# A normalised-attention and two-layer kernel on one core: the SBUF pools put in another order and padded by 832 bytes, so that most large tiles start at a multiple of 2,048 bytes

## The chip, the cores and the metric

The kernel runs on one core of a Trainium2 chip. The metric is the device time of one execution in microseconds (us). TensorE is called PE here, its loading of the stationary operand PEld, VectorE DVE, ScalarE ACT, GpSimd POOL, and SyncE, which issues the transfers, SP. SBUF is the core's working memory: 128 partitions, and a tile has the same byte address in each of them. The addresses of this document are bytes within a partition.

## The reference, cut to what matters

```python
# q, k, v: (4, 6080, 256) float32; w_in (256, 2048), w_out (2048, 256) float64
qn = q / (norm(q, axis=1) + 1e-06)
kn = k / (norm(k, axis=1) + 1e-06)
a = softmax(kn.transpose(0, 2, 1) @ qn / tau)     # 256 x 256 for each of 4 batches
x = (v @ a).reshape(24320, 256)
h = x @ w_in
out = (h - tanh(h)) @ w_out                       # 24320 x 256
```

## The kernel before, in words

**Arithmetic.** The 256 x 256 matrix `a` of a batch is multiplied into `w_in` ("fold", `ps_w`, 12 matmuls for each of 8 column blocks), so that only `v @ (a @ w_in)` is left. Every operand is kept as two float32r parts, a high one and the rest (`vh` and `vl` of v, `gh` and `gl` of h - tanh(h), `f[:, 0]` and `f[:, 1]` of the folded weights, `wo_h` and `wo_l` of `w_out`), and every product is three matmuls: high by rest, high by high, rest by high (`products`, line 267; the six calls of line 868 are two such products). The first two batches' scores `ps_s` are plain float32 matmuls of 256 columns, which the profile lists as two records each; those of batches 2 and 3 are float32r.

**Tiling.** A "quad" is two slices of 512 columns of v (480 in a batch's last pair) by 256 columns of the folded weights. There are 4 batches x 6 pairs x 8 blocks = 192 quads. One quad is a Strassen-like scheme of 7 products, 21 matmuls in which an `f` slice of 128 columns is the stationary operand and a `vh` or `vl` tile moves, and 4 results that each go through tanh, a subtraction and the split into `gh` and `gl`, and then through 6 matmuls with slices of `wo_h` and `wo_l` (24 in all): 45 matmuls. All 192 quads make 8,640, the folds 384, the float32r scores 576: 9,600 float32r matmuls of the 10,034 records on PE.

**Order.** A planner (`Plan.order`) fixes the order of the instructions on every engine from its own cost figures before anything is emitted; it knows rings of buffers (`Ring`), no addresses. `manual_schedule` emits that order. PE takes its matmuls in the written order (`ORDER`, `LAG`), and the other engines work ahead of it within the rings: 3 buffers for `f`, 8 for `vh` and `vl`, 5 for `gh` and `gl`, 3 for `u`, 4 for `c` and `t`, 2 for `ob`, `qh`, `ql` and `nt`, 3 for `raw` and `wi`. All transfers are issued by SP.

**Where tiles lie.** SBUF is handed out in the order in which pools are opened, and in a pool in the order in which tags are first used; each tile is rounded up to 32 bytes. In the program as built, `ident`, the first tile, is at byte 16,512. With tile sizes from the code, everything else follows:

| tiles (bytes each) | PE's use | before: bytes past a multiple of 2,048 | after |
|---|---|---|---|
| `wo_h`, `wo_l` (16,384) | stationary, slices of 512 bytes | 1,216 | 0 |
| `wi` x3 (4,096) | moving, 1,024 bytes | 1,216 | 0 |
| `f` x3 (7,168) | stationary, slices of 512 bytes | 1,216 / 192 / 1,216 | 0 / 1,024 / 0 |
| `raw` x3 (4,096) | first scores | 192 | 0 |
| `nt` x2 (3,040) | none | 192 / 1,184 | 1,024 / 2,016 |
| `qh`, `ql` x2 each (4,096) | both operands of the scores | 128 | 0 |
| `vh`, `vl` x8 each (2,048), `vraw`, `vt` (8,192) | `vh`, `vl` moving, 2,048 bytes | 128 | 0 |
| `eh`, `el` (2,048, in `sm_p`) | stationary in the folds | 352 | 1,184 |
| `u`, `gh`, `gl`, `ob`, `c`, `t` (2,048) | `gh`, `gl` moving, 2,048 bytes | 480 | 0 |

The first matmuls of the program also use `vh`, `vl`, `gh`, `gl`, `qh` and `ql` buffers as landing places for q and k, since these buffers are still empty.

Of the kernel before, what the change touches and what calls it, by code (L numbers as in the profile page):

```python
# [10 lines left out]
F32 = mybir.dt.float32  # L11
F32R = mybir.dt.float32r
I32 = mybir.dt.int32
# [5 lines left out]
P = 128  # L19
GJ = 2  # L20
NMAX = 512
NSQ = 760
# [12 lines left out]
ORDER = [  # L35
    ("p6", []), ("p2", [4, "c"]), ("p5", [2]), ("p7", [3, "a", 6]), ("p4", ["d"]), ("p1", [1]), ("p3", [4, "b", 4]),
]
LAG = 30


# [169 lines left out]
def attn_moe(ctx: ExitStack, tc: tile.TileContext, q, k, vT, qkT, tau, w_in, w_out, outT):  # L210
# [21 lines left out]
    SLOTS = NP * NS2  # L232
    TOTAL = B * SLOTS

    const = ctx.enter_context(tc.tile_pool(name="const", bufs=1))
    w_p = ctx.enter_context(tc.tile_pool(name="w_p", bufs=2))
    f_p = ctx.enter_context(tc.tile_pool(name="f_p", bufs=1))
    qk_p = ctx.enter_context(tc.tile_pool(name="qk_p", bufs=2))
    v_p = ctx.enter_context(tc.tile_pool(name="v_p", bufs=1))
    sm_p = ctx.enter_context(tc.tile_pool(name="sm_p", bufs=1))  # L240
    g_p = ctx.enter_context(tc.tile_pool(name="g_p", bufs=4))
    ps_p = ctx.enter_context(tc.tile_pool(name="ps_p", bufs=1, space=bass.MemoryType.PSUM))
    ring = {
        "wi": Ring(3), "f": Ring(3), "fx": Ring(1), "raw": Ring(3), "qh": Ring(2), "ql": Ring(2), "nt": Ring(2),
# [4 lines left out]
    def sb(pool, tag, shape, dtype, name):  # L249
        return pool.tile(list(shape), dtype, tag=tag, name=name, bufs=ring[tag].bufs)  # L250
# [23 lines left out]

    tau_sb = const.tile([1, 1], F32, name="tau_sb")
    itau = const.tile([P, 1], F32, name="itau")

    ps_tau = []

# [10 lines left out]
    WN = 512  # L290

    class Convert:
# [10 lines left out]
        def magnitude(self):  # L303
            words = self.raw.rearrange("p a (n w) -> p (a n) w", w=2)
            self.low, self.high = words[:, :, 0], words[:, :, 1]
            self.a = sb(qk_p, "nt", [P, NSQ], I32, f"a_{self.name}")[:, 0:WN]
            self.af = self.a.bitcast(F32)

            nc.scalar.activation(self.af, self.high.bitcast(F32), AF.Abs)
# [63 lines left out]
    class Attn:  # L373
# [107 lines left out]
        def load_channels(self, i):  # L481

            row, part = divmod(i, N // NSQ)
            self.channels[i] = sb(qk_p, "nt", [P, NSQ], F32, f"nt_{self.b}_{i}")
            nc.sync.dma_start(
                self.channels[i],
                qkT[row // KC, self.b, row % KC * P:(row % KC + 1) * P, part * NSQ:(part + 1) * NSQ],
            )
# [599 lines left out]
    current = None  # L1088
    lag = LAG

# [70 lines left out]
```

## Time and profile before

| | |
|---|---|
| median of 3 runs | 2247.32 us (2245.41 to 2250.69) |
| the profiled execution's own time | 2247.82 us |
| its span, first to last instruction | 2246.0 us |
| mean granted PE clock | 0.995 |
| PE, PEld, DVE, ACT, POOL busy | 98%, 81%, 78%, 68%, 4% |
| DMA engines busy with the kernel's own queue | 42.9% |

The profile comes from one execution. A group is all instructions of one line, engine, operation and shape, named by its tiles (result first). Matmuls overlap each other in the pipeline, so the length of one (394 ns) is not what it costs: that is the pitch, the time from one matmul's start to the next one's. The chain of waits follows the work that ended last back to the start.

### The profile page before, as it was taken

The page shows a single profiled execution, that of the slowest core. Times are in us where ns is not written, and L with a number is a line of the kernel's source. Part 1 is how long each engine was busy: PE and PEld are TensorE (multiplying, and loading weights), DVE is VectorE, ACT ScalarE, POOL GpSimd, SP SyncE. Part 2 cuts the span into 40 slices and gives each one's busy share as a digit, 9 for nine tenths or more (in the row PEclk, how much of TensorE's full clock was granted, in tenths as well). Part 3 has the DMA queues.
Part 4 walks back from the last instruction along what each step waited for, and adds up shares of the span by engine and source line. Part 5 has one row for each costly group of instructions (what it writes and reads, how often), then busy time and mean ns, then how long its engine had stood idle before and what let it go on. Part 6 is the DMA issues. An engine that isn't in the chain of part 4 may idle for free.

```text
span 2246.0 us, 28772 instructions
## 1 busy us (share of the span) xinstructions
PE 2209.2 (98%) x10034; PEld 1819.5 (81%) x10034; DVE 1750.7 (78%) x2813; ACT 1534.2 (68%) x2770; POOL 79.3 (4%) x62
## 2 busy tenths in 40 slices
PE   8899999999999999999999999999999999999999
PEld 6677778778888888888888888888888888888887
DVE  7688877778788777787788877777778877777775
ACT  6356777776677776776667767777667666666665
POOL 7222000000000000000000000000000000000000
PEclk9899999999999999999999999999999999999999
DMA  9763443443445444444335444444333333332331
GB/s 358 249 217 134 160 161 143 162 149 109 153 163 180 176 150 173 153 161 165 112 138 190 150 175 164 164 176 154 135 122 122 137 129 106 120 117 102 118 118 51
DMA packets 107379, 343.32 MB, mean 153 GB/s; under 512 B 11746, under 2 KB 17378, under 8 KB 107234
## 3 DMA queue, kind: packets, MB, share of 16 engines
q1 hardware_dynamic: 107234, 341.49, 42.9%
q8 instruction: 79, 1.29, 0.2%
q14 instruction: 66, 0.54, 0.1%
HBM read 282.98 MB, written 58.46 MB: 152 GB/s over the span
## 4 chain that ended last, share of the span: by engine, by line
PE 92%; DMA 4%; DVE 2%; issue 1%; ACT 1%; POOL 0%; SPq 0%; DVEq 0%; ACTq 0%; POOLq 0%
PE ps_o L868 46%; PE x L267 23%; PE y L267 11%; PE z L267 6%; PE ps_s L267 4%; PE ps_w L267 2%; DMA outT_dram<-ob 2%; DMA wi<-wi_d 1%; DMA vl<-k_dram 1%; DMA vh<-q_dram 0%; DVE ob L883 0%; DMA gh<-q_dram 0%; DMA vraw<-vT_dram 0%; DMA raw<-q_dram 0%; DMA raw_wi<-w_in_dram 0%
## 5 line engine op out<-in xcount | busy, mean ns | idle before, releaser
L868 PE MATMUL ps_o<-gh,wo_l 128*128 128x512 f32 (+1 forms) x1536 | 604.8, 394 | 4.4 <-DVE ob L883 4.3
L868 PE MATMUL ps_o<-gh,wo_h 128*128 128x512 f32 (+1 forms) x1536 | 605.3, 394 | 0.0
L812 DVE TENSOR_TENSOR gl<-t,gh 128x512 fp32r<-128x512 f32 (+1 forms) x768 | 513.2, 681 | 64.4 <-ACT gh L808 62.0
L808 ACT CAST gh<-t 128x512 fp32r<-128x512 f32 (+1 forms) x768 | 463.0, 618 | 85.1 <-DVE t L804 83.5
L267 PE MATMUL x<-vh,f 128*128 128x512 f32 (+1 forms) x1536 | 478.2, 392 | 1.2 <-DVE f L616 1.2
L868 PE MATMUL ps_o<-gl,wo_h 128*128 128x512 f32 (+1 forms) x1536 | 478.1, 392 | 0.0
L800 ACT ACTIVATE t<-c 128x512 f32<-128x512 f32 (+1 forms) x576 | 361.9, 629 | 166.5 <-DVE c L788 160.8
L804 DVE TENSOR_TENSOR t<-c,t 128x512 f32<-128x512 f32 (+1 forms) x576 | 397.0, 692 | 83.1 <-ACT t L800 73.9
L779 ACT COPY u<-x 128x512 f32<-128x512 f32 (+1 forms) x384 | 223.5, 582 | 235.8 <-PE x L267 235.3
L868 PEld LDWEIGHTS ps_o<-gh,wo_l 128*128 128x128 f32 x1536 | 288.3, 188 | 71.0 <-DVE ob L883 8.0
L267 PEld LDWEIGHTS x<-vh,f 128*128 128x128 f32 x1536 | 288.4, 188 | 66.4 <-DVE f L616 1.7
L868 PEld LDWEIGHTS ps_o<-gl,wo_h 128*128 128x128 f32 x1536 | 288.3, 188 | 61.8
L868 PEld LDWEIGHTS ps_o<-gh,wo_h 128*128 128x128 f32 x1536 | 288.6, 188 | 60.1
L788 DVE TENSOR_TENSOR c<-u,y 128x512 f32<-128x512 f32 (+1 forms) x384 | 260.4, 678 | 86.5 <-ACT u L779 47.4
L267 PE MATMUL x<-vl,f 128*128 128x512 f32 (+1 forms) x768 | 301.7, 393 | 2.1 <-ACT gh L808 1.2
L267 PE MATMUL y<-vh,f 128*128 128x512 f32 (+1 forms) x768 | 238.4, 391 | 0.0
L788 DVE TENSOR_TENSOR c<-p,z 128x512 f32<-128x512 f32 (+1 forms) x192 | 130.8, 681 | 98.9 <-PE z L267 96.9
L804 DVE TENSOR_TENSOR t<-x,t 128x512 f32<-128x512 f32 (+1 forms) x192 | 131.4, 684 | 74.0 <-ACT t L800 72.4
L800 ACT ACTIVATE t<-x 128x512 f32<-128x512 f32 (+1 forms) x192 | 114.0, 594 | 100.9 <-PE x L267 99.4
L267 PEld LDWEIGHTS x<-vl,f 128*128 128x128 f32 x768 | 144.1, 188 | 35.9 <-ACT gh L808 1.6
L267 PEld LDWEIGHTS y<-vh,f 128*128 128x128 f32 x768 | 144.0, 188 | 32.0
L267 PE MATMUL y<-vl,f 128*128 128x512 f32 (+1 forms) x384 | 150.9, 393 | 0.0
(119 smaller groups left out, 2021.8 us busy)
## 6 DMA issues: line engine op xcount, KB each, us to landing
f<-f_d SPq DMA_DIRECT2D x160, 896.0 KB, 4.6
nt<-qkT_dram SPq DMA_DIRECT2D x96, 380.0 KB, 5.6
f_d<-f SPq DMA_DIRECT2D x32, 896.0 KB, 4.5
vraw<-vT_dram SPq DMA_DIRECT2D x80, 256.0 KB, 5.8
outT_dram<-ob SPq DMA_DIRECT2D x80, 256.0 KB, 2.7
raw<-q_dram SPq DMA_DIRECT2D x73, 256.0 KB, 4.9
raw<-k_dram SPq DMA_DIRECT2D x73, 256.0 KB, 5.2
wi<-wi_d SPq DMA_DIRECT2D x30, 512.0 KB, 5.4
```

Source lines behind the costliest of these rows:

```text
L267: ins = nc.tensor.matmul(out, w, x, start=first and i == 0, stop=last and i == len(seq) - 1, skip_group_check=True,)
L779: nc.scalar.copy(self.tiles[to], self.tiles["X"][:, 0:self.n])
L788: nc.vector.tensor_add(self.tiles[i], self.tiles[u], self.tiles[ps][:, 0:self.n])
L800: nc.scalar.activation(self.tiles["t", i], self.tiles[c][:, 0:n], AF.Tanh)
L804: nc.vector.tensor_sub(x, self.tiles[c][:, 0:n], x)
L808: nc.scalar.copy(self.g[i][0], self.tiles["t", i])
L812: nc.vector.tensor_sub(self.g[i][1], self.tiles["t", i], self.g[i][0].bitcast(F32))
L868: nc.tensor.matmul(outs[key + (m,)][:, 0:n], (wo_l if part else wo_h)[:, f, m * P:(m + 1) * P], quad.g[i][x], start=first and j == 0, stop ...
```

## The change: the pools and their order

Three things are done. A tile of 208 float32 (832 bytes) that nothing uses is put behind `itau` in the first pool. The pools are opened in the order `const`, `w_p`, `v_p`, `g_p`, `qk_p`, `f_p`, `nt_p`, `sm_p`. And the tag `nt`, whose 3,040 bytes are no multiple of 2,048, moves out of `qk_p` into a pool of its own. 17,600 + 832 = 18,432 = 9 x 2,048 is then the address of `wo_h`, and the sizes of `w_p` to `fx` are all multiples of 2,048. The middle `f` buffer starts 1,024 bytes past one, because an `f` tile has 3.5 x 2,048 bytes. No instruction is added, removed or moved; no size or number of buffers changes. The last tile ends at byte 228,640 where it ended at 227,808.

```diff
+PAD = 208
...
     const = ctx.enter_context(tc.tile_pool(name="const", bufs=1))
     w_p = ctx.enter_context(tc.tile_pool(name="w_p", bufs=2))
+    v_p = ctx.enter_context(tc.tile_pool(name="v_p", bufs=1))
+    g_p = ctx.enter_context(tc.tile_pool(name="g_p", bufs=4))
+    qk_p = ctx.enter_context(tc.tile_pool(name="qk_p", bufs=2))
     f_p = ctx.enter_context(tc.tile_pool(name="f_p", bufs=1))
-    qk_p = ctx.enter_context(tc.tile_pool(name="qk_p", bufs=2))
-    v_p = ctx.enter_context(tc.tile_pool(name="v_p", bufs=1))
+    nt_p = ctx.enter_context(tc.tile_pool(name="nt_p", bufs=2))
     sm_p = ctx.enter_context(tc.tile_pool(name="sm_p", bufs=1))
-    g_p = ctx.enter_context(tc.tile_pool(name="g_p", bufs=4))
...
     itau = const.tile([P, 1], F32, name="itau")
+    const.tile([P, PAD], F32, name="pad")
...
-            self.a = sb(qk_p, "nt", [P, NSQ], I32, f"a_{self.name}")[:, 0:WN]
+            self.a = sb(nt_p, "nt", [P, NSQ], I32, f"a_{self.name}")[:, 0:WN]
...
-            self.channels[i] = sb(qk_p, "nt", [P, NSQ], F32, f"nt_{self.b}_{i}")
+            self.channels[i] = sb(nt_p, "nt", [P, NSQ], F32, f"nt_{self.b}_{i}")
```

## The prediction, made before the change was run

> **What bounds the kernel now.** I read the page's busy times first, then PE's waits, then the chain of waits, then stretches of the timeline of PE for the pitch, and last the groups and the transfers.
>
> ```profile
> span 2246.0 us, 28772 instructions
> PE 2209.2 (98%) x10034; PEld 1819.5 (81%) x10034; DVE 1750.7 (78%) x2813; ACT 1534.2 (68%) x2770; POOL 79.3 (4%) x62
> ```
>
> PE is idle for 2246.0 - 2209.2 = 36.8 us of the span, and every other engine has slack. What PE waits for (line, releaser, us in total, times, longest):
>
> ```profile
> PE ps_w L267 <- DMA wi<-wi_d: 11.0, 3, 5.0
> PE ps_s L267 <- DMA vl<-k_dram: 6.5, 5, 3.4
> PE ps_o L868 <- DVE ob L883: 4.3, 7, 1.0
> ```
>
> These are the three longest waits, 21.8 us together; the first two lie in the first 180 us. So time can come from PE's pitch, of which there are 9,600 of one kind, or from the start. The chain of waits (start, length, what) gives the pitch of a whole quad. One run of nine `ps_o` matmuls stands in each quad at the same place:
>
> ```profile
> 1803.52 2.10 PE ps_o L868 x9
> 1814.00 2.10 PE ps_o L868 x9
> 1824.49 2.10 PE ps_o L868 x9
> 1834.97 2.10 PE ps_o L868 x9
> ...
> 1950.33 2.10 PE ps_o L868 x9
> ```
>
> The first and the last are 14 quads apart: 146.81 / 14 = 10.486 us a quad, and 10.486 / 45 = 0.2330 us a matmul. So the 160 quads of 512 columns alone are 1,678 us, and a change of 1 ns in the pitch of the 9,600 float32r matmuls is 9.6 us, 0.43% of the span. That is the lever, and all that the change can pull on it is addresses.
>
> **The change part by part.** No instruction, transfer, wait or buffer is added or taken away: the planner knows no addresses, so the order on each engine stays, and the unused tile of 832 bytes issues nothing. The tag `nt` keeps its two buffers, so what waits for a free one stays too. These edits cost 0. What is left is whether an access is dearer or cheaper for the byte at which it starts. Before, nothing large starts at a multiple of 2,048 or even of 256, so the trace can't show the new case itself; but it has five comparisons between different starts.
>
> *First, the start of PE's stationary slices.* The three `f` buffers start 1,216, 192 and 1,216 bytes past a multiple of 2,048, and a quad takes the next one. Slices of 512 bytes that cross a 2,048-byte border in one buffer don't in the next. The four spacings above whose rows are shown are 10.48, 10.49 and 10.48 us, and the 14 of them average 10.486: at most 0.01 us a quad, 0.2 ns a matmul, hangs on the buffer. The rings of five for `gh` and `gl` and of eight for `vh` and `vl` turn as well. For `wo_h` and `wo_l` I take the end, where only `ps_o` is left (start, length, engine, line):
>
> ```profile
> 2233.76 0.38 PE L868 MATMUL ps_o<-gh,wo_l 128*128 128x480 f32 x1
> ...
> 2235.06 0.38 PE L868 MATMUL ps_o<-gh,wo_l 128*128 128x480 f32 x1
> ...
> 2236.37 0.38 PE L868 MATMUL ps_o<-gh,wo_l 128*128 128x480 f32 x1
> ...
> 2237.68 0.38 PE L868 MATMUL ps_o<-gh,wo_l 128*128 128x480 f32 x1
> ...
> 2238.98 0.38 PE L868 MATMUL ps_o<-gh,wo_l 128*128 128x480 f32 x1
> ```
>
> Each row opens a result's six matmuls. The results come in the order 12, 11, 22, 21, 12 here; those of row 1 read slices at 1,216 and 1,728 past a multiple (the second crosses the border), those of row 2 at 192 and 704 (neither does). The spacings are 1.30, 1.31, 1.31 and 1.30 us, with no step between the two kinds. Stationary slices: 0, bounds +-0.01 / 6 us, 1.7 ns, by the rounding of these rows, and +-0.2 ns by the quads.
>
> *Second, the start of PE's moving tiles, in plain float32.* In the first 45 us the scores come out of buffers of three kinds, warm and one after the other:
>
> ```profile
> 21.12 8.80 PE L267 MATMUL ps_s<-gh,gl 128*128 128x256 f32 x40
> 29.76 7.07 PE L267 MATMUL ps_s<-raw 128*128 128x256 f32 x32
> 36.66 5.34 PE L267 MATMUL ps_s<-vh,vl 128*128 128x256 f32 x24
> ```
>
> From start to start: (29.76 - 21.12) / 40 = 0.2160 us at 480 past, (36.66 - 29.76) / 32 = 0.2156 us at 128 past (these `raw` tiles lie in `qh` and `ql`). 352 bytes more or less: 0.4 ns or less.
>
> *Third, the same for float32r.* `vh` and `vl` move from 128 past, `gh` and `gl` from 480 past:
>
> ```profile
> 242.50 2.10 PE ps_o L868 x9
> 244.61 1.40 PE x L267 x6
> ```
>
> 2.10 / 9 and 1.40 / 6 are both 0.2333 us. The rounding of the rows leaves 0.6 + 0.8 = 1.4 ns between them. So a moving tile's start is worth 0, bounds +-1.4 ns on 9,600 matmuls, +-13.4 us. I take 0, because the two starts differ as much from each other as either does from the new one.
>
> *Fourth, both reads at the same place.* After the change stationary and moving operands mostly start at the same byte of a 512-byte stretch; before, they are 64 (`f`, `vh`) and 224 bytes apart (`wo_h`, `gh`). The scores of batches 2 and 3 have had equal starts all along (`qh` against `qh`, or `ql`, 0 apart), and the folds (`wi` at 1,216, `eh` at 352) have 160:
>
> ```profile
> 1007.02 0.28 PE L267 MATMUL ps_s<-ql,qh 128*128 128x256 f32 x1
> ...
> 1007.73 0.39 PE L868 MATMUL ps_o<-gh,wo_l 128*128 128x512 f32 x1
> ```
>
> ```profile
> 1165.02 0.40 PE L267 MATMUL ps_w<-wi,eh 128*128 128x256 f32 x2
> ...
> 1166.45 0.38 PE L868 MATMUL ps_o<-gh,wo_h 128*128 128x480 f32 x1
> ```
>
> 0.71 / 6 = 0.1183 us with equal starts, 1.43 / 12 = 0.1192 us with 160 between: 0.9 ns, and the rounding of the first alone is 1.7 ns. I take 0, bounds +-1.7 ns for 256 columns, so 3.4 ns for 512.
>
> [...]
>
> *Fifth, the other engines and the transfers.* Groups of DVE at three starts (line, tiles, shape, count, busy, mean ns):
>
> ```profile
> L812 DVE TENSOR_TENSOR gl<-t,gh 128x512 fp32r<-128x512 f32 x640 | 431.4, 687 | 53.5 <-ACT gh L808 51.3
> L674 DVE TENSOR_TENSOR vl<-vraw,vh 128x512 fp32r<-128x512 f32 x60 | 41.0, 684 | 0.0
> L463 DVE TENSOR_TENSOR ql<-raw,qh 128x1024 fp32r<-128x1024 f32 x46 | 56.2, 1222 | 6.7 <-ACT qh L456 6.6
> ```
>
> 687 ns with all three tiles at 480, 684 ns with all at 128. 512 columns more cost 535 to 538 ns at mixed starts (192 and 128). Bounds +-3 ns of 687. PE's work covers it: DVE idles 22% of the span; without that cover, 3 ns on 2,813 instructions would be 8 us. For transfers, the issues (tiles, queue, count, KB, median us to landing) and two stretches of the start (busy times of PE, PEld, DVE, ACT, POOL; clock; DMA share; GB/s):
>
> ```profile
> vh<-q_dram SPq DMA_DIRECT2D x14, 256.0 KB, 5.7
> ...
> gh<-q_dram SPq DMA_DIRECT2D x5, 256.0 KB, 6.0
> ```
>
> ```profile
> 15.00:20.00 5.00, 4.99 (x23) 3.90 (x22) 4.62 (x5) 4.40 (x9) 4.92 (x4) 1.00 1.03 388
> ...
> 45.00:50.00 5.00, 4.09 (x20) 3.31 (x19) 4.86 (x5) 4.18 (x9) 4.76 (x4) 1.00 1.05 373
> ```
>
> Between about 5 and 50 us the transfers are at their limit, and there they set PE's pace: this is the one place where a cheaper transfer would count at once. `vh` and `gh` buffers start 128 and 224 bytes past a multiple of 256; 0.3 us of 6 between their landings is 5%, so +-2.3 us on 45 us is the bound. DVE and POOL, busy 4.62 and 4.92 of 5 us in the same stretch, would take part of a gain back. I take 0.
>
> **Sum.** 2247.82 us is the profiled execution's time, 1.8 us above its span and 0.5 us above the median of the three runs. 2247.8 + 0 + 0 + 0 + 0 + 0 - 0.5 = 2247.3 us; predicted 2247 us.
>
> **The rivals.**
>
> *A cheaper start of the moving stream.* The pitch is 0.2330 us at 512 columns and about 0.1185 at 256: (0.2330 - 0.1185) / 256 = 0.447 ns a column, and 4 ns are left that don't grow with the columns. If part of them is paid because tiles start off a border wider than 256 bytes, which no tile of before meets, it goes. By the third comparison that is worth up to 13.4 us; half of it, 6.7 us, gives 2241 us. Against it: starts at 128 and 480 don't differ.
>
> *The whole excess goes.* A plain float32 record takes 0.216 us and moves half the bytes of a float32r one of 0.2330 us. Were the 17 ns between them a price of crooked starts, 7,200 matmuls of 512 columns would save 122 us, 1,440 of 480 (1.305 / 6 = 0.2175 us, against 0.216 x 480 / 512 = 0.2025) 22 us, 960 of 256 about 10 us: 2247 - 154 = 2093 us. Against it: such a price would be paid once a matmul, but the excess grows with the columns, and starts as different as 128 and 480 pay the same.
>
> *Slower: the two reads of PE meet.* PE reads the next stationary slice while the moving tile streams. With both at the same byte of each 512, they could ask for the same part of the memory all along. It would decide from 0.5 ns a matmul (4.5 us in all); at the bound of 3.4 ns on 8,640 matmuls it is 29 us. Half of that, 15 us, gives 2262 us. Against it: the scores of batches 2 and 3, which have equal starts already, are not slower than the folds. For it: at 512 columns no equal start was ever run.
>
> *The change doesn't do what it says.* The tiles may come to lie elsewhere, or the middle `f` buffer, at 1,024 past, may spoil a gain for every third quad. The address sum is 16,512 + 512 + 512 + 32 + 32 + 832 = 18,432 = 9 x 2,048, and all sizes to the last `f` are known. If it failed, the time would be the forecast's.
>
> **How the numbers follow.** No effect 0.62 (its own range 2243 to 2252 us, the bounds of the start's transfers and the spread of the runs); a cheaper start 0.20; the whole excess 0.05; the two reads meet 0.12; other addresses than computed 0.01, at the forecast's time. A measurement of this kernel can tell about 0.2%, 4.5 us, from no change. So faster 0.25, within 0.2% 0.63, slower 0.12. The 80% range takes in most of the cheaper start and the first half of the meeting reads: 2235 to 2257 us; outside lie the 0.05 of the whole excess, some 0.06 of the cheaper start's far end and 0.06 of the slow side.
>
> **What would show it.** The same 28,772 instructions, the quad's spacing of 10.48 to 10.49 us at the same places of the chain, 0.216 us a record for the first scores, and 684 to 687 ns for DVE's groups would show the steps right. A spacing of 10.42 us (0.2316 us a matmul) would be the cheaper start, 9.72 us (0.216) the whole excess, 10.55 us or more the meeting reads. If `x` rows change and `ps_o` rows don't, or the other way, it is the start of `vh` or of `gh`. An unchanged spacing with another total would put the cause into the first 180 us, and would be seen in PE's waits for `wi` and `vl`.

## The result, and the profile after

The changed kernel takes 2214.25 us (median of 5 runs, 2209.88 to 2217.69) where the kernel before takes 2247.32 us (median of 5). The ratio is 0.9849, with a 95% interval of 0.9837 to 0.9861: 1.5% faster. The medians are 33.1 us apart. The profiled execution took 2209.88 us, the fastest of the five, and its span is 37.9 us shorter than that of before. The head of the page of the changed kernel:

```profile
span 2208.1 us, 28772 instructions
PE 2172.0 (98%) x10034; PEld 1820.5 (82%) x10034; DVE 1749.0 (79%) x2813; ACT 1529.5 (69%) x2770; POOL 79.6 (4%) x62
```

The instructions are the same in number, and PEld, DVE, ACT and POOL are busy for the same time within 5 us. PE alone is 37.2 us less busy: the same 10,034 records follow each other more closely. The chain of waits of the changed kernel (start, length, what), at the place in the quad that the prediction used and the six `x` matmuls behind it:

```profile
1805.90 2.04 PE ps_o L872 x9
1807.94 1.36 PE x L270 x6
...
1816.10 2.04 PE ps_o L872 x9
1818.14 1.36 PE x L270 x6
...
1948.70 2.04 PE ps_o L872 x9
```

The last row lies 14 quads behind the first: 142.80 / 14 = 10.200 us a quad, where it was 10.486, and 10.200 / 45 = 0.2267 us a matmul, where it was 0.2330. `ps_o` (2.04 / 9) and `x` (1.36 / 6) both have this pitch. So in these quads 6.4 ns are gone from each matmul of 512 columns, `vh` and `gh` alike.

Not every quad gains so much. A quad that also holds six score matmuls of 256 columns stood 11.17 us behind the one ahead of it, and stands 10.94 us behind it now (before, then after):

```profile
866.10 2.10 PE ps_o L868 x9
877.27 2.10 PE ps_o L868 x9
888.44 2.10 PE ps_o L868 x9
```

```profile
851.44 2.04 PE ps_o L872 x9
862.38 2.04 PE ps_o L872 x9
873.32 2.04 PE ps_o L872 x9
```

That is 0.23 us less, not 0.286. The 32 quads of 480 columns gain next to nothing: five of them take 48.75 us after the change, 9.75 us each,

```profile
2142.18 1.95 PE ps_o L872 x9
...
2190.93 1.95 PE ps_o L872 x9
```

and five took 48.95 us, 9.79 each, before:

```profile
2179.76 1.97 PE ps_o L868 x9
...
2228.71 1.95 PE ps_o L868 x9
```

These samples can't simply be multiplied by 160 wide quads, which would give 37 to 46 us. Both traces have the same 10,034 PE records in the same order, so the spacings can be added up kind by kind: the 7,200 matmuls of 512 columns give 35.3 us of the 37.8 us between the two last starts, 4.9 ns each. The full 6.4 ns come from 1800 to 2100 us; from 110 to 205 us there is no gain at all, and why is open. Of the 37.8 us, 3.6 come in the first 110 us, where waits change too. A little is given back where PE now comes earlier than the copies out of `ps_o` into `ob` that it waits for (PE's waits after; this one was 4.3 us):

```profile
PE ps_o L872 <- DVE ob L887: 7.0, 9, 1.5
```

So nearly all of the gain is PE's pitch in the wide quads. What sets that pitch was the question of the experiments.

### The profile page after: what moved, and what is told of

It reads as the page before. It is cut to its first block, busy times and chain, and to the rows that moved or that the text cites. A ratio compares the mean times of both kernels' runs of the same rounds, so it can differ in the third digit from the quotient of the medians.

```text
span 2208.1 us, 28772 instructions
## 1 busy us (share of the span) xinstructions
PE 2172.0 (98%) x10034; PEld 1820.5 (82%) x10034; DVE 1749.0 (79%) x2813; ACT 1529.5 (69%) x2770; POOL 79.6 (4%) x62
## 4 chain that ended last, share of the span: by engine, by line
PE 92%; DMA 3%; DVE 2%; issue 1%; ACT 1%; POOL 0%; SPq 0%; DVEq 0%; ACTq 0%; POOLq 0%
PE ps_o L872 45%; PE x L270 23%; PE y L270 11%; PE z L270 6%; PE ps_s L270 5%; DMA outT_dram<-ob 2%; PE ps_w L270 2%; DVE ob L887 0%; DMA vl<-k_dram 0%; ACT ob L887 0%; DVE t L808 0%; DMA raw_wi<-w_in_dram 0%; DVE gl L816 0%; DVE acck L424 0%; DMA wi<-wi_d 0%
## 5 line engine op out<-in xcount | busy, mean ns | idle before, releaser
L872 PE MATMUL ps_o<-gh,wo_l 128*128 128x512 f32 (+1 forms) x1536 | 597.7, 389 | 7.2 <-DVE ob L887 7.0
L872 PE MATMUL ps_o<-gh,wo_h 128*128 128x512 f32 (+1 forms) x1536 | 598.2, 389 | 0.0
L270 PE MATMUL x<-vh,f 128*128 128x512 f32 (+1 forms) x1536 | 471.3, 388 | 1.1 <-DVE f L620 1.1
L872 PE MATMUL ps_o<-gl,wo_h 128*128 128x512 f32 (+1 forms) x1536 | 471.6, 388 | 0.0
```

What stands on the lines that cost most here:

```text
L270: ins = nc.tensor.matmul(out, w, x, start=first and i == 0, stop=last and i == len(seq) - 1, skip_group_check=True,)
L872: nc.tensor.matmul(outs[key + (m,)][:, 0:n], (wo_l if part else wo_h)[:, f, m * P:(m + 1) * P], quad.g[i][x], start=first and j == 0, stop ...
```

## The experiments

Three theories of what the change altered for PE stood against each other. DISTANCE: where the stationary slice starts against the moving tile. PLACE: that the moving tile itself starts at a wide border. STATIONARY: that the slices of `wo` and `f` do. The distances of the kernel before, within 256 bytes, are 192 for `vh` (128 past a multiple of 2,048) from `f` (1,216 past), and 32 for `gh` (480) from `wo` (1,216).

### The new order without the unused tile

```diff
-PAD = 208
-    const.tile([P, PAD], F32, name="pad")
```

> The changed kernel without its unused tile of 832 bytes: the pools keep the new order, but all of the large tiles lie 1,216 bytes past a multiple of 2,048, so the distances between them are those of the changed kernel. Theory DISTANCE (what counts is where PE's stationary slice starts against its moving tile, within 512 bytes): as the changed kernel, 10.20 us a quad, about 2214 us. Theory PLACE (what counts is that the moving tile itself starts at a border of 256 bytes or more): as the kernel before, 10.49 us a quad, about 2247 us. Theory STATIONARY (that the slices of wo and f start at a multiple of 512): about 2247 us.

2212.58 us, ratio to before 0.984 (0.9823 to 0.9856). The chain of waits:

```profile
1807.21 2.04 PE ps_o L870 x9
...
1950.01 2.04 PE ps_o L870 x9
```

14 quads in 142.80 us: 10.200 us each, to the last digit the changed kernel's. None of the tiles that PE reads in the quads starts at a multiple of 2,048 or of 256; all lie 1,216 bytes past one of 2,048, the middle `f` buffer 192. PLACE and STATIONARY fall. The unused tile, and with it the multiples of 2,048, does nothing that can be seen.

### The unused tile in the old order

```diff
 (kernel before)
+    const.tile([P, 208], F32, name="pad")
```

> The kernel before with the unused tile alone: wo and f now start at multiples of 512, vh lies 960 and gh 1,312 bytes past a multiple of 2,048, the distances are those of the kernel before. DISTANCE: as before, 10.49 us a quad, about 2247 us. PLACE: as before too. STATIONARY: 10.20 us a quad, about 2214 us.

2247.67 us, ratio 0.9991 (0.9982 to 1.0001).

```profile
1800.38 2.10 PE ps_o L869 x9
...
1957.67 2.10 PE ps_o L869 x9
```

15 quads in 157.29 us: 10.486 us, the kernel before. `wo` and `f` start at multiples of 512 here and it helps nothing, so STATIONARY falls a second time. Both runs agree with DISTANCE.

### All moving tiles shifted by 32 to 256 bytes

In these runs an unused space of so many bytes stands ahead of `vh`, and one that fills it up to 512 bytes ahead of `f`. Stationary slices stay at multiples of 512; the `vh`, `vl`, `gh`, `gl`, `qh` and `ql` tiles, and the tiles of ACT and DVE in the same pools, move together. With 64 bytes:

```diff
 (changed kernel)
+    gap_v = ctx.enter_context(tc.tile_pool(name="gap_v", bufs=1))
+    gap_v.tile([P, 16], F32, name="gap_v_t")
     v_p = ctx.enter_context(tc.tile_pool(name="v_p", bufs=1))
...
+    gap_f = ctx.enter_context(tc.tile_pool(name="gap_f", bufs=1))
+    gap_f.tile([P, 112], F32, name="gap_f_t")
     f_p = ctx.enter_context(tc.tile_pool(name="f_p", bufs=1))
```

> The changed kernel with 64 bytes of unused space ahead of vh, gh and qh, and 448 ahead of f: all moving tiles lie 64 bytes past the borders, all stationary slices stay at multiples of 512. DISTANCE: slower than the changed kernel, 10.3 to 10.5 us a quad, 2225 to 2250 us, if 64 bytes are enough. PLACE: the same. STATIONARY: as the changed kernel, 10.20 us a quad.

2225.4 us, ratio 0.9897 (0.9882 to 0.9912): a third of the gain is lost.

```profile
1807.84 2.06 PE ps_o L876 x9
...
1952.04 2.06 PE ps_o L876 x9
```

14 quads in 144.20 us: 10.300 us. With 32 bytes (and 480):

> The changed kernel with 32 bytes of unused space ahead of vh, gh and qh and 480 ahead of f: every moving tile lies 32 bytes from the stationary slices' borders, the least step that tiles can take. Theory SHORT PERIOD (the distance counts within 64 bytes, so that 224 of the kernel before is the same as 32): the worst case, 231 to 233 ns a matmul, about 2247 us. Theory LONG PERIOD (it counts within 512 bytes and gets worse with the distance): between the changed kernel and 64 bytes, 227 to 229 ns, 2214 to 2225 us.

2256.62 us, ratio 1.0033 (1.002 to 1.0046): slower than the kernel before.

```profile
1810.15 2.10 PE ps_o L876 x9
...
1957.15 2.10 PE ps_o L876 x9
```

14 quads in 147.00 us: 10.500 us, 0.2333 us a matmul. SHORT PERIOD came nearest for this run. With 128 bytes (and 384):

> The same with 128 and 384 bytes. SHORT PERIOD within 64 bytes: as the changed kernel and as 64 bytes, which differ already, so this theory would need a longer period, 128 bytes: then as the changed kernel, 226.7 ns, 2214 us. LONG PERIOD: worse than 64 bytes, 229 to 233 ns, 2225 to 2247 us.

2248.6 us, ratio 1.0003 (0.9993 to 1.0013): nothing of the gain is left, so 128 bytes are no period either, and SHORT PERIOD falls. With 256 bytes (and 256):

> The same with 256 and 256 bytes, the largest distance that 512 allows. A period of 64, 128 or 256 bytes: as the changed kernel, 226.7 ns, 2214 us. LONG PERIOD of 512 bytes: the farthest from it, 231 to 233 ns, about 2247 us.

2212.51 us, ratio 0.9842 (0.9826 to 0.9859).

```profile
1800.16 2.04 PE ps_o L876 x9
...
1953.16 2.04 PE ps_o L876 x9
```

15 quads in 153.00 us: 10.200 us again. 256 bytes are as good as 0; LONG PERIOD falls. Three more distances were run, with 192 (and 320), 224 (and 288) and 96 bytes (and 416):

> The changed kernel with 192 bytes ahead of vh, gh and qh and 320 ahead of f. Theory SYMMETRIC (only how far the two reads are apart around a circle of 256 bytes counts): as with 64 bytes, 229 ns, about 2225 us. Theory ORDERED (it counts which of the two is ahead): another pitch, between 227 and 234 ns.

2250.18 us, ratio 1.0008 (0.9998 to 1.0017). Not the 2225 us of 64 bytes, so SYMMETRIC falls: it counts which of the two starts is ahead.

> The same with 224 and 288 bytes. SYMMETRIC: as with 32 bytes, 233.4 ns, about 2256 us. ORDERED: another pitch; one below 226.7 ns would make this faster than the changed kernel, since 226.7 was the least that any kernel so far held throughout, but single matmuls of 225 ns were seen with 64 and 256 bytes.

2251.97 us, ratio 1.0017 (1.0006 to 1.0028). No distance went below the changed kernel's pitch.

> The same with 96 and 416 bytes. If the pitch grows smoothly with the distance: between 229 (64 bytes) and 232.6 ns (128 bytes), 2225 to 2248 us. If steps of 32 bytes count by themselves, odd ones (32) dear and even ones (64) cheap: about 233 ns, 2250 us or more.

2255.39 us, ratio 1.0026 (1.0016 to 1.0037). The odd step of 32 bytes is dear, as the second reading had it, but so are 128 and 192, which are even. In one table:

| moving tile past the stationary's border, mod 256 | quad without scores, us | ratio to before |
|---|---|---|
| 0 (changed kernel) | 10.200 | 0.9849 |
| 256, that is 0 | 10.200 | 0.9842 |
| 32 | 10.500 | 1.0033 |
| 64 | 10.300 | 0.9897 |
| 96 | 10.500 | 1.0026 |
| 128 | 10.457 | 1.0003 |
| 192 | 10.500 | 1.0008 |
| 224 | 10.500 | 1.0017 |

160 bytes was not run. The ratios of 32 and 192 bytes differ although their wide quads take the same. The traces put more than half of that on the matmuls of 480 columns: from one start to the next (behind 490 us, waits over 265 ns left out) they take 218.9 ns with 32 bytes and 216.2 ns with 192, 3.8 us on all 1,440 of them, of 6.4 us between the medians. At 480 columns a distance of 0, with 216.8 ns, is not the best.

### Only `gh` shifted

With 288 bytes ahead of `g_p` and 224 ahead of `f_p`, `gh` and `wo` stand as in the kernel before, while `vh` and `f` keep their distance of 0:

> The changed kernel with 288 bytes ahead of gh and 224 ahead of f: gh against wo lies as in the kernel before (224 bytes apart within 512), vh against f stays at 0. DISTANCE: only part of the gain is lost, the pitch of ps_o goes up to 232 to 233 ns and that of x stays near 227, some 10.35 us a quad, about 2230 us. PLACE: the same split. STATIONARY: as the changed kernel, 10.20 us.

2246.66 us, ratio 0.9993 (0.9984 to 1.0002). I had expected part of the gain to stay. The chain of waits:

```profile
1800.94 2.10 PE ps_o L876 x9
1803.04 1.39 PE x L274 x6
...
1957.84 2.10 PE ps_o L876 x9
```

15 quads in 156.90 us: 10.460 us. The `x` matmuls run at 1.39 / 6 = 0.2317 us although the distance between their own two tiles is still 0. So DISTANCE, taken matmul by matmul as I had expected it, fails here: one class of moving tiles that is off slows the other too. With 32 bytes (and 480) instead of 288:

> The changed kernel with 32 bytes ahead of gh alone and 480 ahead of f. With 288 bytes here the gain was gone. If 256 bytes are a whole period (64, 128 or 256): the same as with 288, 232.4 ns, about 2247 us. If the period is 512: another pitch than with 288, 227 to 231 ns.

2245.76 us, ratio 0.9991 (0.9982 to 1.0).

```profile
1802.70 2.10 PE ps_o L876 x9
...
1949.14 2.10 PE ps_o L876 x9
```

14 quads in 146.44 us, 10.460 us each: 32 and 288 are the same, a second sign that 256 bytes are a whole turn.

### The old order with three small spaces

```diff
 (kernel before)
+    gap_v.tile([P, 16], F32, name="gap_v_t")     # a pool ahead of v_p, 64 bytes
...
+    gap_g.tile([P, 40], F32, name="gap_g_t")     # a pool ahead of g_p, 160 bytes
...
+    const.tile([P, 16], F32, name="pad")
```

> The kernel before with its pools in the old order and three unused spaces of 64, 64 and 160 bytes (behind itau, ahead of vh, ahead of gh): wo and f, vh, and gh now lie 1,280 (f also 256), 256 and 768 bytes past multiples of 2,048, so all distances are multiples of 256 bytes; no new order, no multiple of 2,048 for the moving tiles. Theory PERIOD 256: as the changed kernel, 10.20 us a quad, about 2213 us. If the new order or the border of 2,048 has a part of its own in the gain: slower than that, up to 2247 us.

2211.35 us, ratio 0.9833 (0.9817 to 0.9849).

```profile
1806.92 2.04 PE ps_o L873 x9
...
1949.72 2.04 PE ps_o L873 x9
```

142.80 us for 14 quads. 288 unused bytes in the kernel before, no new order and no multiple of 2,048 for `wo`, `vh` or `gh`, do all that the change does.

This run holds something else. It is the only one in which the folds, matmuls of 256 columns, have another distance: `wi` at 1,280 and `eh` at 480 are 32 bytes apart (mod 256), where they are 96 apart in all other kernels here. The 12 matmuls of one fold:

```profile
1146.70 0.40 PE L271 MATMUL ps_w<-wi,eh 128*128 128x256 f32 x2
...
1148.10 0.38 PE L873 MATMUL ps_o<-gh,wo_h 128*128 128x480 f32 x1
```

1.40 us, 0.1167 us each, where 12 took 1.43 us, 0.1192 us each, before. Over all folds behind 490 us the mean is 116.8 ns here and 119.3 to 120.1 ns in the other kernels. So at 256 columns the distance seems to count too, and 32 bytes, dear at 512 columns, to be cheaper there than 96; one run is all that shows it.

### What follows, and what stays open

Shown: in these quads the pitch of the float32r matmuls of 512 columns depends, between 10.200 and 10.500 us for 45 of them, on the distance, within 256 bytes, between where the unmoved tiles (`wo`, `wi`, `f`, `fx`) and the moved ones (`vh` to `gl` and their pools) start; no address by itself mattered in the runs that moved all of them together (10.200 us a quad with and without the unused tile in the new order, 10.486 with and without it in the old one). PE reads tiles of both sets in every quad: stationary slices out of `wo` and `f`, moving tiles out of the others. In the quads from 1800 to 1960 us the program lets neither ACT nor DVE touch the unmoved set; only PE and the transfer that brings the next `f` do. Another rival is that ACT's and DVE's work in the moved tiles disturbs PE's reads of the unmoved ones. The starts of single matmuls in the traces, to the nanosecond, speak against it. From 1800 to 1960 us the spacings repeat with 64 bytes every 3 matmuls (229, 231, 226 ns), with 128 bytes every 7, with 192 and 224 bytes every 2, each to within 1 ns through the whole stretch, while the work of ACT and DVE follows the quads of 45. And with 32 bytes the mean from 1760 to 1960 us is 233.5 ns for the 109 matmuls beside which ACT is idle and DVE busy, 233.1 ns for the 30 beside which DVE is idle and ACT busy, and 233.3 ns for the 142 with both busy. So the rhythm is PE's own. That the distance acts between its loading of the next stationary slice and the moving stream, whose busy times overlap (PEld 1820.5 us and PE 2172.0 of the changed kernel's span of 2208.1), is therefore the likely reading, but no run took the loading away, so it isn't shown. Whether the two share anything, and why 64 bytes are cheap (10.300 us) and 32, 96 and 192 dear (10.500) at 512 columns, stays open too.

## Why the prediction was wrong, point by point

**What bounds the kernel** was right: the pitch was the lever, PE the only engine whose busy time fell by more than 5 us, and no instruction or transfer was added.

**The forecast of no effect** was wrong: 2214.25 us lies outside the range, and the chance of 0.63 stood on the wrong case. The terms for DVE and the transfers held: `gl<-t,gh` takes 689 ns after 687, and `vh` and `gh` land in 5.8 and 5.8 us after 5.7 and 6.0. The step that failed is the fourth, both reads at the same place: "I take 0, bounds +-1.7 ns for 256 columns, so 3.4 ns for 512". In its place the runs showed 6.4 ns less a matmul of 512 columns in the undisturbed quads and 4.9 ns on average, 35.3 us in all. It failed through what the first four comparisons compared.

- *First comparison (stationary slices).* The three `f` buffers lie 7,168 bytes apart, which is 28 x 256, and the columns of `wo` 1,024 bytes. All of these starts are the same within 256 bytes. The reading "no step between the two kinds" was right and said nothing of the change.
- *Second (plain float32).* Both operands of those scores come from buffers whose sizes are multiples of 256, in one pool, so their distance was 0 at 480 past as at 128 past. Whether plain float32 matmuls are sensitive to it no run shows.
- *Third (`vh` at 128 against `gh` at 480).* These two did differ in distance: 192 and 32 bytes. The table shows that both happen to be the dearest, 10.500 us a quad each. That two starts "differ as much from each other as either does from the new one" was taken for evidence on the new one; two points of an unknown curve at the same height say nothing of a third. That a moving tile's start by itself is worth 0 turned out right, but this comparison couldn't show it.
- *Fourth (both reads at the same place).* Here the right quantity was named, but measured on matmuls of 256 columns. There the two cases compared, 0 for the scores and 96 (mod 256) for the folds, cost nearly the same, 118.9 and 119.9 ns on average behind 490 us, while at 512 columns 0 and 96 are 6.7 ns apart. Nor does the change alter these distances: six float32r scores go from 0.71 to 0.72 us,

```profile
1000.75 0.28 PE L270 MATMUL ps_s<-ql,qh 128*128 128x256 f32 x1
...
1001.47 0.40 PE L872 MATMUL ps_o<-gh,wo_l 128*128 128x512 f32 x1
```

and the bound drawn from them, 3.4 ns at 512 columns, was too narrow: the real term is 6.4 ns. The price doesn't scale with the columns: in the samples above a quad of 480 columns gains 0.04 us, one of 512 columns 0.286.

**The rivals.** *The meeting reads* named the quantity that decides, with the sign turned round: at 512 columns equal starts are the best of the seven distances run, 10.200 us a quad, not the worst. Unequal starts, 32, 96 and 224 bytes, are the ones that go slower than before (ratios 1.0033, 1.0026 and 1.0017). *A cheaper start of the moving stream* had the direction and a price of up to 13.4 us, some 40% of the 33.1 us between the medians, but its reason, borders wider than 256 bytes, is refuted by the run without the unused tile, 10.200 us a quad with every tile of the quads off such a border. *The whole excess* didn't come: 6.4 of the 17 ns went, and the pitch of 0.2267 us is still 10.7 ns above a plain float32 record's 0.216. The argument against it, that a price of starts is paid once a matmul while the excess grows with the columns, was the second error. The price of the distance is not one and the same for each matmul: 6.4 ns at 512 columns and 0.9 ns (0.04 us / 45) at 480. Why it differs so no run shows.

**What would show it.** The signs of right steps were there for the 28,772 instructions and nearly so for DVE's group (689 ns), but not for the quad's spacing. None of the rivals' spacings came either: 10.200 us lies between the 10.42 of the cheaper start and the 9.72 of the whole excess, and the meeting reads' 10.55 or more was the wrong way. `x` and `ps_o` changed alike, so it was not the start of `vh` or of `gh` alone.

## What to carry to other kernels

Where PE alternates between stationary slices and float32r moving tiles of 512 columns, compute every operand's start address modulo 256 and try all of them on the same remainder; a few unused bytes ahead of a pool do it. Here that took a quad from 10.486 to 10.200 us, and one class of tiles that was off cost the others most of their gain (`x` went from 0.2267 back to 0.2317 us). At 480 columns 192 bytes, with 216.2 ns a matmul, did a little better than 0, with 216.8; at 256 columns the one run with 32 bytes between `wi` and `eh` had 116.8 ns, and the best distance is not known. Comparisons inside one trace can't clear an address effect unless they vary the very quantity that the change varies: work out the addresses of both sides first, and ask what the compared cases have in common. Where no comparison covers the new case, the range has to be wide.

## What the runs showed of the hardware that was not expected

- A float32r matmul of 512 columns with its own weight load had a pitch between 0.2267 us (10.200 / 45) and 0.2333 us (10.500 / 45) at a granted clock of 0.994 to 0.996, by nothing but the distance of start addresses modulo 256. 32 bytes made 3%.
- The pitch is a matter of the whole sequence: with `gh` alone shifted, `x` went from 0.2267 to 0.2317 us with its own tiles in place.
- The recorded length of a stationary slice's loading hardly shows it. With 128 bytes every seventh loading from 1800 to 1960 us takes 192 ns. But in the changed kernel and with 32 bytes the groups have the same mean of 188 ns:

```profile
L872 PEld LDWEIGHTS ps_o<-gh,wo_h 128*128 128x128 f32 x1536 | 288.8, 188 | 53.2
```

```profile
L876 PEld LDWEIGHTS ps_o<-gh,wo_h 128*128 128x128 f32 x1536 | 288.2, 188 | 61.0
```

- Nor are the lengths of single matmuls the pitch, since they overlap: `ps_o<-gh,wo_h` of 512 columns has a mean of 391 ns in the changed kernel and 396 with 32 bytes, at pitches of 226.7 and 233.3. The pitch comes out of the spacing of equal places in the chain of waits, 14 quads apart.
